# A training step of four decode layers: ten instead of nine resident chunks of wo, and 1 MB zero stores from a 2 KB source, on one queue and in other stages

## The chip, the cores and the metric

One core of one Trainium2 chip. The metric is the device time of one execution in microseconds. Most executions of a kernel agree within about 1% here; some fall in a slow state, and comparisons use fast runs only. Profiles are of one execution each, and the span of a profile is about 2 us less than its time.

## The reference, cut

Forward and backward of four layers on one token (D = 1024): A1 (attention over a window of 4096 cached keys), B2 (MLP with Mish, F = 3584), A3 (attention, the same weights as A1), B4 (MLP, the same weights as B2). Outputs are x and the gradients of x, both caches, wq, wo, w1, b1 and w2.

```python
W = min(4096, max(256, Sk // 4))                 # Sk = 32768
k = jnp.repeat(k_cache[:, :, Sk - W:, :], rep, axis=1)
...
x = x + _A_ref(_layernorm(x), A_k_cache, A_v_cache, A_wq, A_wo)
x = x + _B_ref(_layernorm(x), B_w1, B_b1, B_w2)
x = x + _A_ref(_layernorm(x), A_k_cache, A_v_cache, A_wq, A_wo)
x = x + _B_ref(_layernorm(x), B_w1, B_b1, B_w2)
...
_out, _vjp = jax.vjp(_f, A_x, A_k_cache, A_v_cache, A_wq, A_wo, B_w1, B_b1, B_w2)
```

What matters: only the last 4096 of the 32768 rows of a cache are used, so seven eighths of the two cache gradients are zeros. These are 58.7 MB of stores that depend on nothing; the kernel may do them whenever the DMA engines would be idle. The rest of the traffic (weights streamed once per pass, gradients) is tied to the chain of layers.

## The kernel before

The stages in order are A1, B2, A3 forward, B4 forward and backward in one (the "B4 turn"), then A3, B2, A1 backward, then the tail, in which the weight gradients are formed and stored. wq, K, V and the first NR = 9 of 16 chunks of wo stay on chip; the other wo chunks, w1 and w2 are streamed through six slots. Each queue issues in program order: a DMA issued from an engine waits for everything before it on that engine (the GpSimd timeline of the result shows it: a burst issued at 331.00 us, behind a store that had waited 13.96 us).

```python
NB = 6          # slots for streamed tiles
NR = 9          # chunks of wo (512 KB each) that stay on chip
...
    ZC = 2048
    zt = keep.tile([P, ZC], BF16, name="zt")        # 4 KB of zeros per partition
    nc.gpsimd.memset(zt[:], 0.0)
    zero_jobs = []                                  # 112 stores of 512 KB
    per = ZR // P * DH
    for out_t in (out_2, out_3):
        for g in range(G):
            zflat = out_t[0, g, 0:ZR, :].rearrange("(p r) d -> p (r d)", p=P)
            for i in range(per // ZC):
                zero_jobs.append(zflat[:, i * ZC:(i + 1) * ZC])

    def zeros(n):                                   # on the Sync queue
        for _ in range(min(n, len(zero_jobs))):
            nc.sync.dma_start(zero_jobs.pop(0), zt[:])
...
    def bg_zeros(n, after):                         # on the GpSimd queue, after a gate
        if n:
            nc.gpsimd.tensor_copy(gate_t[:], after[:, 0:1])
        for _ in range(min(n, len(zero_jobs))):
            nc.gpsimd.dma_start(zero_jobs.pop(0), zt[:])
... (cut: the layers; wo_load streams chunk c >= NR into one of the six slots)
    # attention backward, the part for A1 (first is False): small copies on GpSimd
    # that lay out the outer products of the tail are taken from prep, one after another
        else:
            after_stream()
            zeros(Z["A1d"])             # all zeros that are left: Sync, behind the last wo load
...
            prep.extend([
                lambda: tall_left("wo", "o", 0),
                ... (cut)
                lambda: row_layout(sA1["dorep"][:].rearrange("p c x -> p (c x)"), "do1"),
                db1_out,
            ])
            nextprep(2)
...
    # how many zeros are issued in which stage
    Z = dict(B2=3, A3=16, B4=[5, 2, 1, 2, 1, 2, 6], A3c=6, A3d=26, W1=3, A1c=3, A1d=36)
```

## Time and profile before

| | before |
|---|---|
| time, median of 3 runs | 451.71 us (450.68 to 451.8) |
| bytes moved | 172.25 MB |
| PE, DVE, ACT busy | 72%, 53%, 50% |
| zero stores | 76 on GpSimd, 36 on Sync, 512 KB each |

The first profile of the kernel before, from which the prediction was read, fell in a slow execution (456.97 us). The lines below are of a second one (450.79 us, span 448.7), which as a single run has no state on record but lies within the fast runs' range. First the page: the span in 40 slices (DMA is the busy share in tenths), the DMA queues (packets, MB, share of the 16 engines' span), the largest GpSimd group and one line of the DMA issues (size, median us to landing).

```profile
span 448.7 us, 11941 instructions
...
DMA  8999997999999999999999999999999999999993
GB/s 317 384 408 425 409 407 293 407 338 343 414 416 392 394 337 305 383 411 415 416 415 415 339 336 360 339 365 419 414 417 419 418 417 417 418 419 419 419 416 161
...
q1 hardware_dynamic: 41120, 131.61, 75.4%
q0 software_dynamic: 11040, 39.86, 22.2%
...
L138 POOL DMA_DIRECT2D out_dram<-zt x76 | 40.6, 537 | 44.3 <-DMA out_dram<-zt 41.7
...
out_dram<-zt SPq DMA_DIRECT2D x36, 512.0 KB, 9.0
```

DMA is the bound: nearly every slice is at nine tenths or more, and the plateau of 414 to 419 GB/s holds from slice 28 (303 us) to the last slice but one. 172.25 MB at 418 GB/s are 412 us of the 448.7. The Trainium skill ("DMA: Bandwidth & Descriptors", section "Specifications") gives a fabric ceiling of 435 GB/s; the highest slice here is 425, the long plateau 414 to 419.

Next, stretches of the same kernel: PE (TensorE's matmuls), PEld (its weight loads), DVE (VectorE), ACT (ScalarE) and GpSimd busy us (with instruction counts), the granted clock of TensorE as a share of full speed, the DMA share (full engines read as about 1.03 here) and GB/s.

```profile
132.00:144.00 12.00, 8.71 (x114) 5.57 (x115) 1.28 (x6) 1.44 (x3) 0.53 (x1) 0.64 1.04 403
144.00:156.00 12.00, 12.00 (x229) 12.00 (x227) 7.73 (x26) 8.59 (x12) 4.05 (x9) 0.77 1.06 387
...
228.00:240.00 12.00, 11.55 (x210) 9.25 (x208) 6.02 (x12) 6.81 (x8) 4.64 (x10) 1.00 1.03 415
...
264.00:276.00 12.00, 9.29 (x175) 9.03 (x176) 5.45 (x14) 4.21 (x5) 2.45 (x6) 0.85 0.99 364
...
324.00:330.00 6.00, 5.11 (x57) 1.56 (x56) 2.79 (x12) 1.01 (x1) 0.71 (x3) 0.75 1.03 416
330.00:336.00 6.00, 3.14 (x27) 2.04 (x28) 2.44 (x10) 1.73 (x2) 0.96 (x5) 0.82 1.03 417
...
400.00:412.00 12.00, 10.09 (x64) 2.17 (x62) 11.89 (x11) 11.33 (x13) 0.00 (x0) 0.50 1.03 418
```

The lines at 324 to 336 are the end of the A1 backward. The chain of layers needs no DMA there, and the DMA engines are full all the same, because of what the Sync queue shows in its timeline (cut at 285 and 345 us, so the first and last counts are of this stretch):

```profile
284.70 11.62 SPq L348 DMA_DIRECT2D wo_c<-in_A_wo_dram  x6
296.38 42.98 SPq L129 DMA_DIRECT2D out_dram<-zt  x36
340.47 4.15 SPq L1058 DMA_DIRECT2D out_dram<-wo_b  x4
```

Sync has nothing else to do between the last wo load (296 us) and the first store of a gradient (340 us), so it feeds 36 zero stores one after another through that whole time.

**A ledger.** Because DMA is the bound, the span can be written as bytes at the plateau rate plus time in which the engines moved less. For each stage, "lost" is its duration less its bytes at 418 GB/s. Stages are cut where DVE writes the layer's input vector or its gradient; bytes are those of the packets that start in the stage. It is worked out from the trace's records, not a view of the profile.

```
kernel before       A1f   B2f   A3f   B4    A3b   B2b   A1b   tail   sum
duration, us        70.1  43.5  31.4  45.5  50.1  51.8  41.4  113.2
MB                  27.5  14.9  12.9  16.1  20.8  18.2  16.7   45.1  172.3
lost, us             4.4   7.8   0.6   6.9   0.4   8.1   1.4    5.2   36.6  (with 1.7 at the very end)
```

### The profile page before, as it was taken

What the parts mean: (1) busy time and instruction counts of PE and PEld (TensorE: products, weight loads), DVE (VectorE), ACT (ScalarE), POOL (GpSimd) and SP (SyncE); (2) the same over time, 40 slices, a digit from 0 to 9 for tenths busy, and PEclk for the clock granted to TensorE, in tenths of its full rate; (3) what the DMA queues carried; (4) which work ended last, traced back from release to release, by engine and by line L of the source; (5) the groups of instructions that cost most, each with busy time, mean ns of one, the idle gap of its engine ahead of it and who ended that gap; (6) DMA issues with size and microseconds to landing.
All of it is one profiled execution on the core that took longest, in us unless ns stands there. A gap on an engine that the chain in (4) does not pass through costs nothing.

```text
span 454.9 us, 11941 instructions
## 1 busy us (share of the span) xinstructions
PE 324.7 (71%) x5107; PEld 224.4 (49%) x5107; DVE 236.6 (52%) x489; ACT 225.2 (50%) x262; POOL 56.6 (12%) x146
## 2 busy tenths in 40 slices
PE   0566854497896968985999888977868679897300
PEld 0334524387566968974687888844631111121000
DVE  3124101197422736683344874572359889999400
ACT  1122100075332837777365553536329899989400
POOL 2000000001422111341242002042010000000000
PEclk9997565578967969997879557999975555555555
DMA  8999997999999978999999799999999999999994
GB/s 323 385 412 422 407 409 281 381 322 370 417 416 384 404 238 282 354 392 411 419 413 414 273 362 349 321 400 417 415 417 420 418 416 417 419 418 419 419 420 172
DMA packets 52257, 172.25 MB, mean 379 GB/s; under 512 B 5200, under 2 KB 12396, under 8 KB 51180
## 3 DMA queue, kind: packets, MB, share of 16 engines
q1 hardware_dynamic: 41120, 131.61, 74.5%
q0 software_dynamic: 11040, 39.86, 22.0%
q8 instruction: 40, 0.66, 0.5%
q14 instruction: 13, 0.11, 0.1%
q10 hardware_dynamic: 44, 0.01, 0.0%
HBM read 72.89 MB, written 98.58 MB: 377 GB/s over the span
## 4 chain that ended last, share of the span: by engine, by line
PE 21%; ACT 12%; DMA 7%; issue 4%; SPq 3%; DVE 3%; DVEq 0%; POOL 0%; ACTq 0%; POOLq 0%
PE ops L229 7%; PE tps L193 7%; ACT wq_b L148 6%; DMA w_c<-in_B_w_dram 4%; PE acc L229 3%; SPq L129 3%; DMA wo_c<-in_A_wo_dram 2%; ACT st_o L148 2%; DMA out_dram<-zt 1%; ACT wo_b L148 1%; ACT K L148 1%; ACT V L148 1%; PE d L229 1%; PE tps L623 1%; ACT wo_c L148 1%
## 5 line engine op out<-in xcount | busy, mean ns | idle before, releaser
L138 POOL DMA_DIRECT2D out_dram<-zt x76 | 40.4, 536 | 44.5 <-DMA out_dram<-zt 41.9
L229 PEld LDWEIGHTS <-w_c 128*128 128x128 bf16 x1120 | 37.3, 103 | 16.7 <-DMA w_c<-in_B_w_dram 13.4
L633 ACT COPY w_c<-tps 128x1024 bf16<-128x1024 bf16 x28 | 28.2, 1012 | 21.7 <-PE tps L623 11.8
L229 PE MATMUL ops<-V 2*128 2x512 bf16 (+1 forms) x160 | 34.8, 598 | 5.9 <-ACT wq_b L148 3.4
L647 DVE CUSTOM_DVE_ANT_0 scr<-w_c,gbc 128x1024 bf16<-128x1024 bf16 x28 | 34.2, 1220 | 4.3 <-DMA w_c<-in_B_w_dram 2.2
L145 DVE CAST wq_b<-ops 128x1024 bf16<-128x1024 f32 (+1 forms) x31 | 33.8, 1148 | 3.8 <-PE ops L229 3.2
L148 ACT CAST wq_b<-ops 128x1024 bf16<-128x1024 f32 (+1 forms) x33 | 33.7, 1140 | 2.2 <-PE ops L229 2.0
L148 ACT COPY K<-tps 128x1024 bf16<-128x1024 bf16 x19 | 18.7, 1029 | 30.2 <-PE tps L193 30.2
L229 PE MATMUL ops<-wo_b 2*128 2x512 bf16 x120 | 23.3, 567 | 10.9 <-ACT wq_b L148 7.2
L229 PEld LDWEIGHTS <-V 128*128 128x128 bf16 (+2 forms) x416 | 14.2, 102 | 27.8 <-issue 27.6
L623 PE MATMUL tps<-ident_bf,w_c 128*128 128x128 bf16 x224 | 24.5, 276 | 1.1 <-DMA w_c<-in_B_w_dram 0.7
L148 ACT COPY w_b<-tps 128x1024 bf16<-128x1024 bf16 x20 | 19.5, 1015 | 6.7 <-PE tps L193 6.7
L145 DVE COPY K<-tps 128x1024 bf16<-128x1024 bf16 x13 | 8.9, 690 | 25.8 <-PE tps L193 25.8
L193 PE MATMUL tps<-ident_bf,K 128*128 128x128 bf16 x256 | 22.1, 252 | 0.1
L229 PE MATMUL q<-wq_b,nA_pair 128*32 128x512 bf16 x128 | 11.2, 440 | 15.0 <-DMA wq_b<-in_A_wq_dram 14.9
L193 PEld LDWEIGHTS <-K 128*128 128x128 bf16 x256 | 18.6, 115 | 4.5 <-issue 4.4
L813 DVE CUSTOM_DVE_ANT_0 wo_c<-wo_c,gbc 128x1024 bf16<-128x1024 bf16 x14 | 16.4, 1217 | 8.0 <-DMA wo_c<-in_A_wo_dram 4.3
L229 PEld LDWEIGHTS <-wo_b 2*128 2x128 bf16 (+1 forms) x152 | 5.6, 99 | 29.3 <-issue 28.6
L623 PEld LDWEIGHTS <-w_c 128*128 128x128 bf16 x224 | 18.5, 124 | 1.7 <-issue 0.9
L148 ACT CAST K<-ops 128x1024 bf16<-128x1024 f32 x18 | 17.7, 1014 | 2.5 <-PE ops L229 1.8
L193 PE MATMUL tps<-ident_bf,w_c 128*128 128x128 bf16 x224 | 17.1, 236 | 2.3 <-DMA w_c<-in_B_w_dram 2.3
L193 PE MATMUL tps<-ident_bf,wq_b 128*128 128x128 bf16 x256 | 18.0, 238 | 1.0 <-issue 1.0
(323 smaller groups left out, 651.9 us busy)
## 6 DMA issues: line engine op xcount, KB each, us to landing
out_dram<-zt POOLq DMA_DIRECT2D x76, 512.0 KB, 10.6
out_dram<-zt SPq DMA_DIRECT2D x36, 512.0 KB, 10.3
wo_c<-in_A_wo_dram SPq DMA_DIRECT2D x28, 512.0 KB, 8.4
w_c<-in_B_w_dram SPq DMA_DIRECT2D x32, 448.0 KB, 6.4
w_c<-in_B_w_dram SPq DMA_DIRECT2D x28, 512.0 KB, 6.0
out_dram<-wq_b SPq DMA_DIRECT2D x17, 512.0 KB, 11.4
wq_b<-in_A_wq_dram SPq DMA_DIRECT2D x16, 512.0 KB, 11.6
out_dram<-K SPq DMA_DIRECT2D x8, 1024.0 KB, 12.7
```

Of the source, the lines that this page charges most:

```text
L129: nc.sync.dma_start(zero_jobs.pop(0), zt[:])
L138: nc.gpsimd.dma_start(zero_jobs.pop(0), zt[:])
L145: nc.vector.tensor_copy(out_ap, in_ap)
L148: nc.scalar.copy(out_ap, in_ap)
L193: nc.tensor.transpose(ps[:, b, :], ap, ident_bf[:])
L229: nc.tensor.matmul(out_ap, lhsT=lhsT, rhs=rhs, start=start, stop=stop, skip_group_check=True, **kw)
L623: nc.tensor.transpose(self.ps[c][:, b, :], w[:, 1, b * P:(b + 1) * P], ident_bf[:])
L633: nc.scalar.copy(self.w[c][:, 1, :], self.ps.pop(c)[:].rearrange("p b c -> p (b c)"))
L647: nc.vector.tensor_tensor_reduce(out=scr[:], in0=w[:, 0, :], in1=gbc[:], scale=1.0, scalar=0.0, op0=ALU.mult, op1=ALU.add, accum_out=self. ...
L813: nc.vector.tensor_tensor_reduce(out=w[:, 0, :], in0=w[:, 0, :], in1=gbc[:], scale=1.0, scalar=0.0, op0=ALU.mult, op1=ALU.add, accum_out=w ...
```

## The change

The intent was to move fewer bytes (a tenth wo chunk stays on chip, paid for by smaller constants: a 2 KB zero source read four times per row, no `pat`, a one-column `ones1`), to keep Sync for loads alone by putting every zero store on the GpSimd queue in 56 pieces of 1 MB, and to move zeros away from the w2 and w1 loads of the B2 backward. The core of the diff:

```diff
-NR = 9
+NR = 10
...
-    ZC = 2048
-    zt = keep.tile([P, ZC], BF16, name="zt")
+    ZC = 4096
+    zt = keep.tile([P, ZC // 4], BF16, name="zt")
     nc.gpsimd.memset(zt[:], 0.0)
+    zt2 = zt[:, None, :].to_broadcast([P, 4, ZC // 4])
...
-                zero_jobs.append(zflat[:, i * ZC:(i + 1) * ZC])
-
-    def zeros(n):
-        for _ in range(min(n, len(zero_jobs))):
-            nc.sync.dma_start(zero_jobs.pop(0), zt[:])
+                zero_jobs.append(zflat[:, i * ZC:(i + 1) * ZC].rearrange("p (a b) -> p a b", a=4))
...
-            nc.gpsimd.dma_start(zero_jobs.pop(0), zt[:])
+            nc.gpsimd.dma_start(zero_jobs.pop(0), zt2)
...
     def row_layout(col32, name):
-        ps = psum1([P, P], BF16, "rps")
-        nc.tensor.transpose(ps[:, 0:P], col32[:], ident_bf[:])
+        ps = psum1([P, P], FP32, "rps")
+        for c in range(NC):
+            mm(ps[32 * c:32 * c + 32, 0:P], col32[:], ident_bf[:], True, True, tile_position=(0, 32 * c))
...
+            if i == 4:                                  # B2 forward, fifth w1 load
+                gbc = bcast_row(g_bf)
+                bg_zeros(Z["B2a"], n_bf)
...
             after_stream()
-            zeros(Z["A1d"])
...
             nextprep(2)
+            bg_zeros(Z["A1d"], None)                    # A1 backward
...
             rows_put(area["Rq"], 1, "dq", "heads")
+            bg_zeros(Z["A1e"], None)                    # end of A1 backward
...
-    Z = dict(B2=3, A3=16, B4=[5, 2, 1, 2, 1, 2, 6], A3c=6, A3d=26, W1=3, A1c=3, A1d=36)
+    Z = dict(B2a=1, B2={NW2 - 2: 1}, A3=6, B4=[0, 1, 1, 1, 1, 1, 2], A3c=3, A3d=15, B4w={}, W1=0, A1c=6, A1d=5, A1e=100)
... (cut: smaller constants, warm-up matmuls in gaps, order of the late wo chunks)
```

The numbers in Z count stores, of 512 KB before and of 1 MB after.

> **What bounds the kernel now.** The 16 DMA engines. The slices view shows 418 to 420 GB/s from 300 to 444 us, and the same plateau in 108-138 and 198-250; the queue view shows 172.25 MB, 412 us at 418 GB/s for a span of 455. The rest is idle DMA time. By 12 us slices of the packet records: 3 us at the start, 7 in the B2 forward (60-114; the rate falls to 32 GB/s at 72, while PE waits for the broadcast and all six streaming slots are full), 8 in the B4 turn (156-198; 107 GB/s at 162-168, where PE waited 4.5 us for a w1 block queued among zero stores), 9 in the B2 backward (250-300), 6 to 7 at the end. In the tail DVE and ACT are 90% busy until 425, but stores land until 449.
>
> **What the change does.**
> 1. Ten wo chunks stay: 24 streamed loads instead of 28, 2.1 MB less: -5 us at 418 GB/s. Six streamed chunks fit six slots, so no seventh load waits for a slot; the one in the A3 backward cost 9.35 us in the chain of waits (200.8-210.2), the one in the A3 forward 3.6 us of PE (timeline). These stages get 2 to 4 us shorter, but they are DMA-full, so zeros slide into the tail; this gains only the bytes.
> 2. Zeros: 56 of 1 MB, all on GpSimd; 33 MB instead of 36 before the last attention backward. A3 and B4 get 13 MB instead of 18: w1 blocks come sooner and the 4.5 us stall should go. 1 MB more in the B2 forward, at the idle hole: -2.5 us. None in the B2 backward's w1 part. The Trainium skill ("DMA: Bandwidth & Descriptors", section "Issuing engines are not separate DMA queues") says the queues interleave on the same 16 engines; the trace agrees (300-312 us: 279 and 131 GB/s, together about 412). So another queue gains nothing of itself.
> 3. The 2 KB source. Packets took 309 ns for 8 KB, 159 for 4 KB, 46 for 1 KB: about 9 ns plus bytes at 27.3 per ns. The w1 blocks (1 KB rows in HBM, 4 KB in SBUF) appear as 1 KB packets and reach only about 360 GB/s alone. If zeros likewise go as 2 KB packets (estimate 84 ns, from that line), 58.7 MB cost 8 us more engine time, part of it in idle time; if as 8 KB, 4 us less. I think 2 KB likelier, 60 to 40.
> 4. Small: matmuls in the gaps to keep the clock (0.50 in 250-276), four small matmuls for one with `pat`: +-1 us; DVE was as busy there.
>
> **Sum.** 451.7 - 5 (bytes) - 5 (less idle DMA: B2 forward, B4, B2 backward) = 442; +6 with 2 KB packets, -4 with 8 KB. Predicted 443.0 us, range 435 to 450. Chances: faster by over 2% 0.48, within 2% 0.48, slower 0.04.
>
> **What shows it.** Queue view: 170.1 MB, 24 loads of wo_c. GpSimd's packets: 2 KB near 84 ns or 8 KB near 309; the plateau where zeros run alone (before: 415). No 9 us wo_c wait in the chain; B2 backward starts 10 us earlier; no hole after the first B4 blocks; 70-75 us filled; DMA full from the last attention backward to the end.
>
> **What would make it wrong.** GpSimd blocks at eight outstanding 1 MB stores and holds up copies that PE waits for; 18 MB of zeros from the A3 backward spill over the B2 backward's w2 loads; 2 KB packets slow the loads beside them; B4 stays as long with fewer bytes.

## The result, and the profile after

The time after is 469.6 us, median of 4 runs (465.85 to 471.63), beside 451.75 (450.68 to 453.37) for the kernel before: a ratio of 1.0382, 95% interval 1.0309 to 1.0455. The kernel became 3.8% slower; the prediction had been 443.0 us and had given "slower by over 2%" 4%. Here and below a ratio is the mean time of one kernel's fast runs over that of the other's in the same rounds, so not quite the ratio of the medians quoted.

The page after, with the lines that answer to those above:

```profile
span 467.4 us, 12004 instructions
...
DMA  8999999999997999999999889997599999999998
GB/s 323 389 411 415 407 406 335 411 333 340 417 324 236 353 343 396 344 411 417 383 382 363 312 278 348 390 369 277 194 380 388 392 392 400 403 403 405 407 406 323
...
q1 hardware_dynamic: 35504, 111.16, 62.6%
q0 software_dynamic: 15328, 58.74, 33.0%
...
L136 POOL DMA_DIRECT2D out_dram<-zt x56 | 42.5, 764 | 36.3 <-DMA out_dram<-zt 33.8
...
out_dram<-zt POOLq DMA_DIRECT2D x56, 1024.0 KB, 16.4
```

Three things are new in the two rows of slices. Slices 28 and 29 (315 to 339 us) fall to 277 and 194 GB/s where before the plateau had begun. Slices 12 and 13 (129 to 152 us) fall to 324 and 236. And from slice 30 to the last but one, where DMA is nine tenths busy again, the rate is 380 to 407, not 418: full engines, fewer bytes. The same stretches as before:

```profile
132.00:144.00 12.00, 9.64 (x157) 6.65 (x156) 3.00 (x12) 3.41 (x8) 0.00 (x0) 0.77 0.90 295
144.00:156.00 12.00, 12.00 (x291) 12.00 (x289) 9.05 (x35) 10.48 (x14) 1.88 (x4) 1.00 0.72 238
...
228.00:240.00 12.00, 12.00 (x204) 9.16 (x201) 5.92 (x15) 6.32 (x8) 0.63 (x1) 1.00 1.02 376
...
264.00:276.00 12.00, 11.49 (x211) 11.32 (x211) 6.34 (x13) 5.22 (x7) 0.78 (x2) 0.73 0.78 265
...
324.00:330.00 6.00, 4.37 (x70) 1.79 (x62) 3.11 (x12) 1.34 (x2) 0.08 (x1) 0.90 0.06 22
330.00:336.00 6.00, 2.64 (x19) 2.29 (x19) 2.06 (x9) 1.01 (x1) 6.00 (x12) 0.67 0.61 211
...
400.00:412.00 12.00, 1.17 (x12) 0.42 (x15) 2.41 (x3) 1.97 (x3) 0.00 (x0) 0.50 1.02 405
```

The DMA share separates the two kinds of loss. At 144 to 156 it is 0.72, at 264 to 276 it is 0.78, and at 324 to 330 it is 0.06: for part of the time, or nearly all of it, the engines had nothing to do. At 228 to 240 and at 400 to 412 it is 1.02, as before, and yet the rate is 376 and 405 where it was 415 and 418: each packet took longer. The packet records of the trace say by how much. The median 4 KB packet took 159 ns before in each of the following stretches; after, it took 159 ns at 120 to 130 us, 174 at 222 to 240, 171 at 342 to 355 and 162 at 400 to 430.

The hole at 324 us is explained by the timeline of GpSimd, in program order (in brackets: idle time before, and what ended it; the view is cut at 336 us, the last burst has 12 stores in all):

```profile
291.08 4.50 POOL L136 DMA_DIRECT2D out_dram<-zt  x6
295.63 1.80 POOL L1118 MEMSET wo_b<- 128x2048 bf16 x1
...
302.60 3.73 POOL L136 DMA_DIRECT2D out_dram<-zt  x5
306.33 1.20 POOL L1010 COPY wo_b<-o_pair 128x16 bf16<-128x16 bf16 x8
313.25 0.60 POOL L1020 COPY wo_b<-gA_pair 128x8 bf16<-128x8 bf16 x4 [5.72 <-PE rw L977]
315.49 0.47 POOL L987 COPY wo_b<-nA_pair 128x32 bf16<-128x32 bf16 x2 [1.64 <-PE rw L977]
329.92 0.54 POOL L1215 DMA_DIRECT2D out_dram<-wo_b  x1 [13.96 <-DVE wo_b L1214]
330.45 0.65 POOL L990 COPY wo_b<-dq_pair 128x16 bf16<-128x16 bf16 x4
331.00 5.25 POOL L136 DMA_DIRECT2D out_dram<-zt  x7
```

Eleven stores of 1 MB are issued by 306 us, and their last packet ends at 325.8. The next ones stand in GpSimd's program behind copies that wait for PE and DVE, the last of them 13.96 us, and are issued at 331.00. Sync, which had covered this time before, sits idle:

```profile
288.39 0.76 SPq L350 DMA_DIRECT2D wo_c<-in_A_wo_dram  x1
338.17 7.04 SPq L1062 DMA_DIRECT2D out_dram<-wo_b  x6
```

The ledger shows that the loss is in the bytes left over, not in the chain of layers:

```
kernel after        A1f   B2f   A3f   B4    A3b   B2b   A1b   tail   sum
duration, us        70.2  43.8  28.9  45.3  51.6  50.5  44.8  130.8
MB                  27.5  15.3  10.7  15.1  20.0  16.7  13.7   51.5  170.7
lost, us             4.4   7.0   3.3   9.1   3.7  10.5  12.0    7.5   59.1  (with 1.6 at the very end)
```

The last attention backward starts at 290.2 us (292.4 before), so the chain was ahead by 2.2 us; the first output product starts at 336.1 (334.6), 1.5 us behind. But 51.5 MB were left for the tail instead of 45.1. In sum, 1.6 MB less are worth -3.8 us at 418 GB/s, and 22.5 us more were lost: +18.7 us of span, which is the difference of 467.4 and 448.7.

### The profile page after: what moved, and what is told of

The parts are those of the page before. It is cut to its first block, busy times and chain, and to the rows that moved or that the text cites. A ratio compares the mean times of both kernels' runs of the same rounds, so it can differ in the third digit from the quotient of the medians.

```text
span 467.4 us, 12004 instructions
## 1 busy us (share of the span) xinstructions
PE 318.6 (68%) x5180; PEld 214.6 (46%) x5180; DVE 234.3 (50%) x484; ACT 225.2 (48%) x262; POOL 58.0 (12%) x125
## 2 busy tenths in 40 slices
DMA packets 50928, 170.66 MB, mean 365 GB/s; under 512 B 4256, under 2 KB 11452, under 8 KB 49852
## 3 DMA queue, kind: packets, MB, share of 16 engines
q0 software_dynamic: 15328, 58.74, 33.0%
## 4 chain that ended last, share of the span: by engine, by line
DMA 20%; PE 14%; ACT 7%; issue 5%; DVE 5%; POOL 1%; DVEq 0%; SPq 0%; ACTq 0%; POOLq 0%
DMA out_dram<-wq_b 6%; PE tps L191 6%; DMA out_dram<-st_o 5%; DMA w_c<-in_B_w_dram 4%; DMA out_dram<-K 3%; PE acc L227 3%; ACT K L146 2%; DMA out_dram<-wo_b 2%; ACT wq_b L146 2%; DVE scr L647 2%; PE ops L227 1%; PE sm L227 1%; PE d L227 1%; ACT wo_c L146 1%; ACT wo_b L146 1%
## 5 line engine op out<-in xcount | busy, mean ns | idle before, releaser
L136 POOL DMA_DIRECT2D out_dram<-zt x56 | 42.5, 764 | 36.3 <-DMA out_dram<-zt 33.8
L227 PEld LDWEIGHTS <-w_c 128*128 128x128 bf16 x1120 | 35.6, 101 | 24.7 <-DMA w_c<-in_B_w_dram 18.5
L143 DVE CAST wq_b<-ops 128x1024 bf16<-128x1024 f32 (+1 forms) x29 | 31.6, 1151 | 3.5 <-PE ops L227 3.0
L146 ACT CAST wq_b<-ops 128x1024 bf16<-128x1024 f32 (+1 forms) x31 | 31.8, 1137 | 2.2 <-PE ops L227 2.0
L143 DVE CAST K<-ops 128x1024 bf16<-128x1024 f32 x14 | 16.6, 1222 | 13.2 <-DMA out_dram<-K 12.4
L623 PE MATMUL tps<-ident_bf,w_c 128*128 128x128 bf16 x224 | 20.9, 249 | 0.7 <-DMA w_c<-in_B_w_dram 0.7
L227 PE MATMUL acc<-a_pair,w_c 128*128 128x16 bf16 x448 | 15.5, 171 | 7.0 <-DMA w_c<-in_B_w_dram 6.9
L191 PE MATMUL tps<-ident_bf,K 128*128 128x128 bf16 x256 | 20.0, 239 | 0.0
L191 PEld LDWEIGHTS <-K 128*128 128x128 bf16 x256 | 17.2, 109 | 3.8 <-issue 3.7
L191 PE MATMUL tps<-ident_bf,w_c 128*128 128x128 bf16 x224 | 17.4, 239 | 1.9 <-DMA w_c<-in_B_w_dram 1.9
L146 ACT COPY w_c<-tps 128x768 bf16<-128x768 bf16 (+1 forms) x14 | 11.6, 830 | 13.1 <-PE tps L191 13.1
```

The lines of the kernel that those rows point to most:

```text
L136: nc.gpsimd.dma_start(zero_jobs.pop(0), zt2)
L143: nc.vector.tensor_copy(out_ap, in_ap)
L146: nc.scalar.copy(out_ap, in_ap)
L191: nc.tensor.transpose(ps[:, b, :], ap, ident_bf[:])
L227: nc.tensor.matmul(out_ap, lhsT=lhsT, rhs=rhs, start=start, stop=stop, skip_group_check=True, **kw)
L623: nc.tensor.transpose(self.ps[c][:, b, :], w[:, 1, b * P:(b + 1) * P], ident_bf[:])
```

## The experiments

All results were correct. The expectations name theories by letters. A is that slow packets come from where tensors lie on chip, at first in the form of a common shift by 32 bytes; its main rival is the hole in the A1 backward; later letters are further guesses at what makes the packets slow (the early store, the schedule, the number of chunks). The time of the kernel before, from the same rounds, stands in brackets; medians are of all runs, ratios of fast runs alone. Lost time is from the ledger of each profile.

### r_before: the kernel before, unchanged

> The kernel before, unchanged, for a profile in the fast state on the same chip as the next three. All theories: 450 to 454 us, a plateau of 415 to 420 GB/s where zeros run alone and in the tail, 4 KB packets at a median of 159 ns.

Measured: 450.79 us (449.86). This is the clean profile shown above. It showed that one reading of the prediction was of the slow execution only. The first profile had this line in its PE timeline, and 107 GB/s at 162 to 168 us:

```profile
162.84 0.60 PE L229 MATMUL sm<-nB_pair,w_b 128*128 128x16 bf16 x16 [4.50 <-DMA w_b<-in_B_w_dram]
```

In the clean profile no PE wait of 3 us or more stands there, and the same stretch moved 313 GB/s. The "4.5 us stall" that the change was to remove was not part of the 451.7 us.

### s_shape: before, with only the shape of the zeros changed

```diff
-    ZC = 2048
-    zt = keep.tile([P, ZC], BF16, name="zt")
+    ZC = 4096
+    zt = keep.tile([P, ZC // 4], BF16, name="zt")      # 1 MB stores, 2 KB source, Z halved
```

> The kernel before with the zero stores alone changed: 56 of 1 MB with 8 KB destination rows from a 2 KB source, in the same places and on the same queues (counts halved). If the shape is what makes zeros slow (in the changed kernel's profile their packets take a median of 173 to 178 ns where they run alone, against 159 before), this kernel loses about 58.7 MB x 9%, some 10 to 13 us: 460 to 465 us. If the queue, the schedule or the ten wo chunks are to blame, it stays within 3 us of before: 449 to 455 us, packets at 159.

Measured: 452.38 us (449.86), 1.0037 [0.9999, 1.0075]; packets of zeros 159 to 160 ns on the GpSimd queue. So neither 1 MB stores nor the 2 KB source cost more than 0.8%. From GpSimd the zeros appear as 4 KB packets, on Sync as 2 KB packets of about 84 ns (405 to 407 GB/s at 312 to 348 us).

### t_sp_tail: after, with the last zeros back on Sync

```diff
             after_stream()
+            zeros(Z["A1d"])                 # 17 stores on Sync, behind the last wo load
...
-            bg_zeros(Z["A1d"], None)
...
-            bg_zeros(Z["A1e"], None)
```

> The changed kernel with the 17 MB of zeros of the last attention backward (the two bursts after the first six stores) back on the Sync queue, behind the last wo loads, as before. If bursts on GpSimd leave the hole at 324 to 336 us (8.6 us idle) and stretch the last attention backward by 6 us, this recovers 10 to 15 us: 455 to 459. If the shape is to blame, the hole goes but slow zero packets stay: 458 to 463. If neither matters: 468 to 471.

Measured: 459.27 us (449.86), 1.0193 [1.0163, 1.0223]. The same stretches as above:

```profile
324.00:330.00 6.00, 5.07 (x71) 2.07 (x68) 2.23 (x9) 1.60 (x2) 0.00 (x0) 0.81 1.03 377
330.00:336.00 6.00, 2.95 (x24) 2.45 (x24) 2.10 (x9) 1.01 (x1) 1.17 (x5) 0.76 1.04 382
```

The hole is gone: the loss of the A1 backward fell from 12.0 to 2.8 us, and half of the slowdown with it. It is not all: the rate with full engines is 377 to 382, and the stages before are as starved as in the changed kernel (A3 backward 3.1, B2 backward 12.0 us lost).

### h_half: after, with 112 zero stores of 512 KB

```diff
-    ZC = 4096
-    zt = keep.tile([P, ZC // 4], BF16, name="zt")
+    ZC = 2048
+    zt = keep.tile([P, ZC // 2], BF16, name="zt")     # and every count of Z doubled
```

> The changed kernel with zeros of 512 KB (4 KB destination rows, still from a 2 KB source), counts doubled, same places, all on GpSimd. If 8 KB destination rows are slow, packets go back to 159 ns and 8 to 12 us are recovered: 457 to 462. If the 2 KB source is slow, or SBUF placement, or the schedule, nothing is recovered: 466 to 473. GpSimd may now block at eight outstanding stores of half the size in the last attention backward, which would cost some us there.

Measured: 475.46 us (449.86), 1.0554 [1.0524, 1.0583]. Smaller stores made it worse, by 1.7%. The A1 backward lost 18.1 us instead of 12.0. GpSimd waits whenever eight of its stores are under way (that is the group's "idle before, DMA out_dram<-zt" in the page), so with stores of half the size half as many bytes are queued when it turns to its copies. In the traces of r_before, after and h_half no store is issued with more than seven others under way, and in the profile after all waits of 1.3 to 4.4 us come at that count. There is a second cause in this run: twice as many stores take GpSimd longer to issue (0.72 us each; the first 12 of this stage from 290.8 to 300.5 us), and PE waited 6.8 us for the copies behind them, where the changed kernel has 1.7. Here the stores did hold up copies that PE waits for, and the A1 backward took 50.4 us instead of 44.8. The size of a store on that queue is an advantage of the change, not a fault.

### pad32, sp_pad32, b_shift32: a shift of all tensors by 32 bytes

The compiled programs showed that the smaller constants had moved the large tensors: zt lies at a multiple of 512 bytes in the partition before, 32 bytes past one after; wq and wo moved from 32 to 64, K and V from 256 to 288. The three kernels shift everything by an unused tile of 32 bytes.

```diff
+    shift = keep.tile([P, 1], FP32, name="shift")     # takes 32 bytes
+    nc.vector.memset(shift[:], 0.0)
```

> The changed kernel with one unused 32-byte tile first in the pool, so that every later tile stands 32 bytes further (zt, K and V again at a multiple of 64 bytes, wq_b, wo_b and the streaming slots again 32 bytes past one, as in the kernel before). All kernels made from the changed one have slow packets (zeros 170 to 178 ns, tail stores 162 to 166, 406 GB/s against 419), none made from the kernel before has. Theory A, SBUF placement: packets go back to 159 ns, tail to 418 GB/s; some 13 us of slow packets are won, the hole at 324 to 336 us grows by some 3: 457 to 463 us. Rival B, the other contents of the change (ten chunks, schedule, single queue): 467 to 471, packets stay slow.

> The same 32-byte shift in the kernel with the tail zeros back on Sync (459.3 us, no hole). Theory A: 447 to 452 us, tail at 418 GB/s. Rival B: 457 to 461.

> The kernel before with the same unused 32-byte tile (and one 64-byte tile folded into another's place to make room), so that its tiles stand as the changed kernel's do: zt, K, V 32 bytes past a multiple of 64, wq_b, wo_b and slots at a multiple. Theory A: slow packets appear in a kernel that has nothing else of the change: 457 to 463 us, tail at 404 to 408 GB/s. Rival B: 449 to 452.

Measured: after with the shift (pad32) 470.41 us (451.7), 1.0403 [1.0326, 1.0481], its profile in the slow state; t_sp_tail with it (sp_pad32) 458.49, 1.0168 [1.0124, 1.0212]; the kernel before with it (b_shift32, where another small tile had to share a buffer to make room) 452.52, 1.0017 [0.9947, 1.0086]. The theory in this form fell: one more shift by 32 repairs nothing, and the kernel before hardly minds one, although its stores in the tail did drop to 404 to 408 GB/s. Its zeros, read from a 4 KB source 32 bytes past a multiple of 512, stayed at 159 ns.

### fillhole: pad32 with four stores moved into the hole

```diff
+            bg_zeros(Z["A1x"], None)                  # A1x=4, after the next piece of prep
```

> pad32 with four of the last twelve zeros issued earlier, between the second and the last burst on GpSimd, to fill the hole. Theory A with the hole as the second cause: 8 to 10 us less than pad32, 449 to 453 us. If the hole were only a symptom (the tail bound by evacuation), as pad32. GpSimd may block at eight outstanding stores and delay its copies by 1 to 3 us.

Measured: 462.7 us (451.7), 1.0239 [1.0172, 1.0306]: 1.6% better than pad32 in the same rounds (7.4 us between the means of fast runs), still all on GpSimd. The A1 backward lost 5.5 us. So most of the cost is not the queue, but that its last stores stand behind the copies; sp_pad32, with these stores on Sync, is at 1.0168, and the two intervals overlap.

### x_noearly, x_oldsched, x_nr9: the schedule of the zeros, and NR

All three start from t_sp_tail. x_noearly moves the one early store of the B2 forward to where the other one is; x_oldsched gives every stage what it had before; x_nr9 has nine resident chunks.

```diff
 # t_sp_tail:
 Z = dict(B2a=1, B2={NW2 - 2: 1}, A3=6, B4=[0, 1, 1, 1, 1, 1, 2], A3c=3, A3d=15, B4w={}, W1=0, A1c=6, A1d=17)
 # x_noearly:
+Z = dict(B2a=0, B2={NW2 - 2: 2}, A3=6, B4=[0, 1, 1, 1, 1, 1, 2], A3c=3, A3d=15, B4w={}, W1=0, A1c=6, A1d=17)
 # x_oldsched:
+Z = dict(B2a=0, B2={NW2 - 2: 2}, A3=8, B4=[2, 1, 1, 1, 0, 1, 3], A3c=3, A3d=13, B4w={}, W1=1, A1c=2, A1d=18)
 # x_nr9:
-NR = 10
+NR = 9
```

> The changed kernel with its tail zeros on Sync (459 us), and its first zero store, which stood in the B2 forward before the first w2 load, moved behind that stage's loads; the program then touches its DRAM tensors in the order of the kernel before. Theory C, the early store (or the order of the tensors it brings): zeros where they run alone at 220 to 250 us go back to 159 ns and 415 GB/s: 449 to 454 us. Otherwise: 458 to 461, zeros at 170 to 176 ns there.

> The same with the zero schedule of the kernel before in every stage (counts halved, tail on Sync); what is left of the change is ten chunks, the smaller constants, the clock-keeping matmuls and the later broadcast. Theory D, the schedule (8 MB queued at once from the A3 backward, none in the B4 turn's first block, none in the B2 backward's w1 part): 445 to 450 us, 2 MB fewer loads showing as some 5 us. If the rest of the change slows the packets: 456 to 461.

> The changed kernel with its tail zeros on Sync, but nine chunks instead of ten. Theory E, the tenth chunk (its SBUF, or six instead of seven streamed chunks) makes packets slow: they go back to 159 ns, and 450 to 456 us in spite of 2 MB more loads. Otherwise packets stay slow and the 2 MB cost 3 to 5 us: 461 to 465.

Measured, with 453.58 us for the kernel before: x_noearly 454.2 us, 1.0019 [0.995, 1.0089]; x_oldsched 448.4, 0.9876 [0.9815, 0.9936]; x_nr9 462.75, 1.0213 [1.0141, 1.0284]. So the schedule of the zeros, which the prediction had booked as a gain, is most of what was left of the slowdown: moving one store out of the B2 forward's w1 loads is worth 1.7%, and giving all stages their old amounts back another 1.4% (the A3 forward and the B4 turn get more, the A3 backward 13 instead of 15, and the backward stages after it change a little too). What these stores fill is seen at 144 to 156 us, in t_sp_tail first, then in x_oldsched:

```profile
144.00:156.00 12.00, 11.81 (x281) 11.69 (x279) 9.69 (x36) 10.48 (x13) 1.88 (x4) 1.00 0.66 216
```

```profile
144.00:156.00 12.00, 8.37 (x164) 8.04 (x162) 5.20 (x19) 5.70 (x9) 1.57 (x3) 0.86 1.05 385
```

In t_sp_tail PE is all but full here and the DMA engines have work for two thirds of the time. The loads come early, as the prediction said; but the time won is less than the bytes left out: the A3 forward and the B4 turn together move 25.8 MB instead of 29.0, a difference of 7.7 us at 418 GB/s, but take 74.2 us instead of 76.9, only 2.7 us less. The zeros that would have filled the gap have to be stored in the tail. In x_oldsched PE waits more and the engines are full. With DMA as the bound, that is the cheaper way round. (In this pair the ledger does not place the gain in these two stages alone: they lose 9.2 us in x_noearly and 8.8 in x_oldsched, of 42.0 and 39.0 in all. The pair with fast packets below does.) The packets stayed slow in all three (380 to 385 GB/s at 324 to 348 us in x_oldsched), which took the schedule and the number of chunks off the list of their causes. The tenth chunk by itself is not resolved: x_nr9 and t_sp_tail differ by 0.2%, within both intervals.

### b_early: the kernel before, with one of its zeros early

```diff
+            if i == 4:
+                bg_zeros(1, n_bf)             # and B2=3 becomes B2=2
```

> The kernel before with one of its three B2 zeros moved to the fifth w1 load of the B2 forward, so that the DRAM tensors are touched in the changed kernel's order. Theory C: slow zeros appear (170 to 176 ns at 220 to 250 us), 456 to 461 us. Otherwise 448 to 452.

Measured: 450.77 us (453.58), 0.9912 [0.9844, 0.998], packets as fast as before. The early store does not make packets slow, and one of 512 KB in this place does no harm; it even gained a little. Theory C fell with it.

### place_old, place_zt, place_after, place_noearly: tensors put back where they were

place_old is x_oldsched with zt, wq, wo, K, V and the streaming slots at the addresses modulo 512 of the kernel before (0, 32, 32, 256, 256, 480); place_zt is x_oldsched with zt alone moved to a multiple of 512; place_after and place_noearly are the changed kernel and x_noearly with all places of before. The part that moves zt:

```diff
+    ZC = 4096
+    zt = keep.tile([P, ZC // 4], BF16, name="zt")     # allocated first, ahead of onesD's old place
...
-    ZC = 4096
-    zt = keep.tile([P, ZC // 4], BF16, name="zt")
```

> x_oldsched (0.988 of before, slow packets) with zt, wq_b, wo_b, K, V and the slots at the remainders by 512 of the kernel before (0, 32, 32, 256, 256, 480), by allocating three small tiles elsewhere. If placement makes the packets slow: zeros and tail back to 159 ns and 418 GB/s, 5 to 8 us won, 0.970 to 0.978 of before. Otherwise 0.985 to 0.991, packets slow.

> x_oldsched with the zero source alone moved to a multiple of 512. If it is the source's place that slows zeros: zeros at 216 to 250 us back to 159 ns and 415 GB/s, the tail's other stores still at 404 to 408, 0.980 to 0.986. If placement is of no account: 0.985 to 0.991.

> The changed kernel with all of these places. If placement makes the packets slow: A3 backward and tail at 415 to 419 GB/s, but the faster zeros leave a longer hole before the last burst; 1.020 to 1.032 of before. Otherwise 1.035 to 1.042.

> x_noearly (1.002 of before: the change's schedule without the early store, tail zeros on Sync) with all of these places. If placement makes the packets slow: 0.983 to 0.992. Otherwise 0.998 to 1.006.

Measured in 3 rounds (place_old in 5), with 452.04 us for the kernel before: place_old 443.05 us (442.51 to 445.95), 0.9817 [0.9788, 0.9846]; place_zt 443.43, 0.9813 [0.9785, 0.984]; place_after 463.87, 1.0254 [1.0207, 1.0301]; place_noearly 450.45, 0.9995 [0.9945, 1.0045]. For the speed of the packets the place of the zero source is enough. The same two stretches, first of x_oldsched, then of place_zt:

```profile
228.00:240.00 12.00, 11.72 (x193) 8.53 (x191) 6.02 (x14) 6.19 (x7) 0.00 (x0) 1.00 1.02 382
...
348.00:360.00 12.00, 8.32 (x46) 1.60 (x42) 10.73 (x11) 11.18 (x12) 0.00 (x0) 0.50 1.02 406
```

```profile
228.00:240.00 12.00, 11.99 (x197) 8.79 (x194) 6.00 (x14) 6.31 (x7) 0.00 (x0) 1.00 1.02 413
...
348.00:360.00 12.00, 6.54 (x38) 1.18 (x36) 9.65 (x10) 10.64 (x10) 0.00 (x0) 0.50 1.02 418
```

Same share of busy engines, same work, 382 against 413 GB/s. The median packet at 222 to 240 us is 160 ns in place_zt and place_old, against 174 in the changed kernel. In the last part of the tail place_zt falls back a little (408 to 411 GB/s from about 408 us), place_old does not (419 to 420).

In time the placement shows less. place_old (expected 0.970 to 0.978) falls between its two expectations. place_zt has the time that was expected, but its tail recovered too (418 GB/s), where 404 to 408 had been expected. place_noearly had its packets back at 160 ns and still landed in the range for "otherwise": 0.2% from x_noearly, with overlapping intervals. Only the step from the changed kernel to place_after, 1.3%, has intervals that do not overlap.

These runs also give the size of the other two causes with fast packets: place_noearly to place_old, 1.8% for the amounts per stage (the A3 forward and the B4 turn lose 12.2 us in place_noearly and 6.1 in place_old, of 38.6 and 32.4 in all); place_after to place_noearly, 2.6% for the early store and the hole together.

### s_zt32, place_early: two terms that rested on one comparison each

s_zt32 is s_shape with only zt moved 32 bytes off a multiple of 512 (a 32-byte tile before it, 480 bytes behind, so that everything else keeps its place). place_early is place_old with one of the two B2 stores early.

```diff
 # s_zt32, from s_shape
+    pad_a = keep.tile([P, 16], BF16, name="pad_a")
     zt = keep.tile([P, ZC // 4], BF16, name="zt")
+    pad_b = keep.tile([P, 240], BF16, name="pad_b")
 # place_early, from place_old
-    Z = dict(B2a=0, B2={NW2 - 2: 2}, A3=8, ...
+    Z = dict(B2a=1, B2={NW2 - 2: 1}, A3=8, ...
```

> The kernel before with 1 MB zeros from the 2 KB source (as s_shape), the source alone moved 32 bytes off a multiple of 512; all other large tensors keep their place modulo 512. Placement theory (the place of the zero source alone is enough): packets of zeros that run alone 167 to 177 ns after the B2 forward where s_shape had 159 to 160, the tail's stores at 404 to 410 GB/s, time 1.008 to 1.02 of the kernel before. Rival 1 (the place of the source matters only with the changed kernel's other contents): packets as in s_shape, time 1.00 to 1.006. Rival 2 (slow packets cost no time where something else bounds): packets slow, time within 1.006.

> place_old with one of its two 1 MB zeros of the B2 forward moved to the fifth w1 load; nothing else. If the early zero is what cost t_sp_tail its 1.7% against x_noearly: 0.990 to 1.000 of the kernel before, B2 forward 1.5 to 3 us longer than place_old's 40.8 us. If it was the placement or the number of zeros in the B2 forward together with the rest of the schedule: 0.978 to 0.985, B2 forward within 0.7 us of 40.8.

Measured, with 451.42 us for the kernel before: s_zt32 457.01 us, 1.0104 [1.0021, 1.0186]; place_early 446.97, 0.9886 [0.9818, 0.9955]. The two stretches of s_shape, then of s_zt32:

```profile
240.00:252.00 12.00, 11.45 (x237) 9.48 (x230) 6.25 (x14) 4.84 (x5) 0.00 (x0) 0.86 0.86 334
...
348.00:360.00 12.00, 7.54 (x40) 1.37 (x38) 10.59 (x11) 10.65 (x11) 0.00 (x0) 0.50 1.03 418
```

```profile
240.00:252.00 12.00, 11.26 (x242) 8.80 (x240) 6.11 (x14) 5.33 (x6) 0.00 (x0) 1.00 0.76 289
...
348.00:360.00 12.00, 8.65 (x42) 1.61 (x42) 11.46 (x11) 11.18 (x12) 0.00 (x0) 0.50 1.03 396
```

So in the old program, too, moving the 2 KB source by 32 bytes and nothing else brings slow packets. The time is 1.0104 against 1.0037 for s_shape, in different jobs with overlapping intervals, so that it costs time is not shown by this pair. The packets: 172 ns for the median zero packet at 240 to 252 us where s_shape has 160, and 396 GB/s with full engines at 348 to 360 us. They are fewer than in the changed kernel (the median at 222 to 240 us is still 160 ns, with a quarter of the packets at 175 or more at 228 to 240 us). At 120 to 130 us they are at 159 ns in both, as they are in the changed kernel: the slowing begins only after that.

place_early lies between its two expectations: 0.7% slower than place_old, in another job and with overlapping intervals. Its B2 forward takes 44.5 us instead of 40.8 and loses 1.4 us more, and the B4 turn loses 1.7 us more. The early store of 1 MB costs something or nothing here; it did not gain.

## Why the prediction was wrong

The mechanism that it relied on was right: the kernel is DMA-bound, and time is bytes plus DMA time that is not used. It mis-stated the second term.

1. **The step that failed is "DMA full from the last attention backward to the end", and with it "-5 (less idle DMA: B2 forward, B4, B2 backward)".** In its place the runs showed 22.5 us more lost DMA time, 10.6 of them in the A1 backward; and the three stages in which 5 us less had been booked lost 26.6 us instead of 22.8. Taking the last zeros off GpSimd alone brought 1.0382 to 1.0193. The prediction had listed that "GpSimd blocks at eight outstanding 1 MB stores and holds up copies that PE waits for"; in the changed kernel it was the other way round (PE waited for these copies twice, 1.7 us each; only in h_half did such a wait grow). The copies, in order on the same engine and waiting for PE and DVE, held up the stores. The Trainium skill ("DMA: Bandwidth & Descriptors", section "Issuing engines are not separate DMA queues") says that DMAs of all issuing engines interleave on the same 16 engines and that the choice saves only issue time. The trace agrees on bandwidth, and the prediction drew from it that moving the queue costs nothing. But the choice of engine also decides what the issue stands behind: here the engines ran dry at 325.8 us and the next burst was issued at 331.00.

2. **"A3 and B4 get 13 MB instead of 18: w1 blocks come sooner and the 4.5 us stall should go."** The blocks came sooner and PE was full at 144 to 156 us, but the stall had only been in the slow execution, and the B4 turn took 45.3 us instead of 45.5. The 0.66 to 0.72 DMA share there is 5 us of lost DMA time in A3 forward and B4 that the tail had to pay. Going back to the old amounts per stage was worth 1.4% (x_noearly to x_oldsched) and 1.8% (place_noearly to place_old, where the ledger finds 6.1 of the 6.2 us won in these two stages).

3. **"1 MB more in the B2 forward, at the idle hole: -2.5 us."** The stretch at 72 to 84 us did fill (363 GB/s instead of 326; place_old reaches 376 there without the early store), but against t_sp_tail leaving the early store out gained 1.7%, and against place_old putting it in cost 0.7%, not resolved from zero. It gained 0.9% only as 512 KB in the old kernel. The stage that it was to fill became longer: the B2 forward takes 43.8 to 45.5 us in the nine profiles of kernels made from the changed one that have the early store, and 40.8 to 42.2 in the five that do not. Why the sign of the whole depends on the rest of the schedule is open.

4. **The 2 KB source.** The prediction weighed 2 KB packets near 84 ns against 8 KB packets near 309. From GpSimd they were 4 KB packets: 58.74 MB in 15328 packets. The same skill page (section "SWDGE vs HWDGE vs iDMA") says that a packet is preferably at most 4096 B; that agrees and speaks against 8 KB, but it would not have told 4 KB from 2 KB, which the same stores show on Sync. The shape by itself cost at most 0.8% (s_shape 1.0037 [0.9999, 1.0075]). What cost was where the source came to lie: by the way of the smaller constants it moved 32 bytes off a multiple of 512. Moving it back was worth 1.3% from the changed kernel to place_after, where the other tensors were moved too, 0.6% from x_oldsched to place_zt and 0.2% from x_noearly to place_noearly; the last two are not resolved from zero. That a 159 ns packet could become one of 174 was nowhere in the prediction.

5. **The bytes.** "2.1 MB less: -5 us" was mis-sized: four loads fewer, but one resident chunk more to load, so 1.6 MB (172.25 to 170.66), -3.8 us at 418 GB/s.

6. **What held.** 24 streamed loads; the wait for a wo_c load of 7.56 us in the chain (9.35 in the first profile) is gone in the chain after; the start of the last attention backward came 2.2 us earlier. The B2 backward did not start 10 us earlier, as the prediction's list of signs has it: its gradient was written at 239.7 us instead of 240.6. (In the slow first profile, from which the sign was read, it is written at 249.9; against that one the sign would have seemed to come true.)

7. **The intent was sound.** place_old has the ten chunks, the 1 MB stores and the 2 KB source, and gains 1.8%: 443.05 us. Its ledger loses 32.4 us instead of 36.6, so 4.2 us less idle DMA and 3.8 us of bytes, close to the -5 and -5 of the prediction. That it equals the predicted 443.0 us is partly luck: place_old has neither the early store nor the new amounts per stage to which the prediction booked its -5, and the B2 backward, one of the three stages named for it, lost no less than before (8.5 us, 8.1 before).

The steps as ratios to the kernel before: after 1.0382; last zeros on Sync 1.0193; no early store 1.0019; old amounts per stage 0.9876; zero source at a multiple of 512 0.9813. They are partly from different jobs, on different chips, and their intervals reach 0.3 to 0.7% to each side. Neighbours have intervals that do not overlap, but for the last two: that step is shown by the packets and not by the time.

What stays open: by what mechanism the place of the zero source slows stores, also those of other tensors in the tail, and why it comes and goes: no profile shows it before 124 us, and in the changed kernel the zeros are back at 159 to 160 ns from 156 to 186 us. The same skill page (section "How a descriptor splits into AXI transactions") says that a descriptor which does not start at a multiple of 256 B needs an extra transaction and fetches unused bytes. The direction agrees, and zt is the tensor that had been aligned. The size does not: an estimate from that section is 65 beats instead of 64 for 2 KB starting 32 B past such an address, 1.6%, where 159 to 174 ns are 9%. Nor does the pattern: wq and wo lie at 32 in the kernel before and stores from them take 159 ns, b_shift32 reads a misaligned 4 KB source at 159 ns, and the changed kernel itself does so at 120 to 130 us. No run tells multiples of 256 from multiples of 512. Nor is it shown why the tail of b_shift32 is slower while its time hardly moves.

## What to carry to other kernels

Work that fills idle DMA time belongs on a queue that has nothing else to wait for; on an engine that also does copies, look at what stands in front of it in program order, and follow the bytes to the stage where they end up. When DMA is the bound, starving it to let a compute stage run ahead only moves bytes to the end. And when full DMA engines move fewer bytes than before, compare packet times and the addresses of the sources: freeing a few hundred bytes of constants can shift every tensor behind them.

## What the Trainium skill lacked or had wrong

- "DMA: Bandwidth & Descriptors", section "Issuing engines are not separate DMA queues": right on bandwidth, but the section lacks that a store stands behind the issuing engine's other work. Here that left the engines at 22 GB/s at 324 to 330 us; putting the last zeros on Sync was worth 1.9%.
- The same page, section "How a descriptor splits into AXI transactions": counted in beats, it explains about 1.6% (estimate above) for a 2 KB read that starts 32 B off; the runs show packets of 174 ns instead of 159, slower packets also for other stores later in the same program, and 0.2 to 1.3% of the time (only the 1.3% resolved). Nor does it say that the same shift left a 4 KB source at 159 ns (b_shift32).
- The same page, section "SWDGE vs HWDGE vs iDMA": a packet of at most 4096 B agrees with GpSimd's zeros (2 KB source, 8 KB destination rows, 4 KB packets of 159 ns). It does not say that the same store from Sync appears as 2 KB packets of about 84 ns, at 405 to 407 GB/s instead of 413 to 417.
- No page has that in programs built like these GpSimd waits when eight of its stores are under way, so that the size of a store decides how many bytes are queued. 512 KB instead of 1 MB took the ratio from 1.0382 to 1.0554, in part by that and in part by the longer issuing of twice as many stores.
